# A three-round token-mixing kernel: crossbar transposes issued from ScalarE, rows of x added at an earlier visit, later chunks convolved one step sooner

## The chip, the cores and the metric

The kernel runs on one core of one Trainium2 chip. The metric is device time in microseconds, from the first to the last work of one execution. Timed runs give a median; a profiled execution gives the trace that is read below. Engines are named as the profile names them: PE (TensorE), DVE (VectorE), ACT (ScalarE), POOL (GpSimd), SP (SyncE, which here only issues DMAs).

## The reference

A causal convolution with softmax weights along the sequence is followed by a mixing block. B is 8, S is 4224, D is 192, there are 8 heads of 24 channels and 7 taps.

```python
w = softmax(weight, axis=-1)                      # 8 heads x 7 taps
x = einsum('hk,bskhg->bshg', w, windows_of(x))    # causal window of 7 tokens
theta = x @ w_theta
zr, zi = x * cos(theta), x * sin(theta)
y = einsum('ts,bsd->btd', w_tok_r, zr) + einsum('ts,bsd->btd', w_tok_i, zi)
u = x + y
out = u + maximum(u @ w_ch, 0)
```

Almost all of the arithmetic is in the two 4224 x 4224 token matrices, each multiplied with a 4224 x 1536 operand (8 batches of 192 channels).

## The kernel before, in words

**Tiles.** The sequence is cut into 33 chunks of 128 source tokens (index k) and 33 blocks of 128 target tokens (tb). Batch and channel together are one row of N = 1536 values. A chunk's operand z has seven pieces of 768 columns, since the two token products of a pair of target blocks are computed with seven products in place of eight (a Strassen-like scheme; T1, T2, T3 and T4 are differences of the cosine and sine products).

**Rounds and steps.** 11 chunks (NW) are resident at a time. There are 58 steps. A step works on one pair of target blocks (every seventeenth step on a single one) with all resident chunks. Seventeen steps (NU) visit all target blocks once and the steps go round them a little over three times, so each target block is visited three or four times; between visits its partial sum `pv` is stored in HBM (`part`) and loaded again (`load_rows`, L346). The last visit of a block is its final one. Chunks of the next round replace those of the last one gradually: chunks 11 to 21 enter at steps 18 to 23, chunks 22 to 32 at steps 36 to 41.

**A step.** `mix` (L404) runs seven products ("runs") one after another; each run is 2 matmuls of 384 columns for each resident chunk (L417). With 9 chunks a run has 18 matmuls, with 11 it has 22. After each run `give` (L374) adds the PSUM result to `pv` on DVE (L382); in the first round part of it is copied by ACT (L380). The PSUM results live in tiles `y`, of which there are two buffers.

**The hand-written order.** All other work is a list of events with positions from 0 to 7 within the step, where the integer part is the run. `mix` emits an event when the matmul at that position comes. Each engine executes its instructions in the emitted order (`pe`, `dve`, `act`, `pool` tie each to the one before). DMAs that SP issues, and those of `load_chunk`, are ordered by the tile framework. Events that matter here:
- `w_tasks` (L335): for the following step, four 32x32 block transposes of weight tiles (`turn`, L317) and four sums of them (`wsum`, L329) on DVE, into `wt` tiles with 10 buffers.
- `load_w` (L297): POOL loads the weights of the step after next, with a cast to fp16.
- `load_chunk` (L272): x of a chunk into `xw`, from POOL, and a halo of earlier tokens from SP (L183). `xw` and `pv` share six buffers (tag `big`).
- `conv` (L197): the convolution by PE (L205) in two halves, each evacuated by ACT; x then lies in pieces T2 and T4 of the chunk's z tile and is also stored in HBM as `xs` (L222).
- `transpose` (L226): for each half, six PE transposes (L162) and an evacuation by ACT (L148).
- `theta` (L231): the channel mix by PE (L138), then cosine and sine by ACT (L242). `product` (L247) and `sums` (L253) on DVE finish z.
- `add_x` (L358): before a final visit, the row of x is added to `pv`. Usually SP loads the row into `xr` (L363) and POOL adds it (L364). For some steps (`ahead`) POOL instead issues accumulating DMAs from `xs` to `part` some steps before (L369).
- `outputs` (L456): after a final visit each block is cast to fp16 in two halves (`cast`, L436, ACT), transposed (`turn_u`, L440), mixed with w_ch by PE (L138), joined by DVE (L446) and stored (L451). In steps 41 to 52 the transpose is a crossbar DMA that SP issues (L156); in the last five steps (`late`) PE does it. Times in `outputs` are microseconds relative to the step's end, by the planner's own reckoning of a step.

For a chunk of a later round all ten of its tasks (two convolutions, two transposes, two thetas, two products, two sums) stand in the one step before it enters, at positions 0.1 to 3.7 for the first chunk of a pair and 2.3 later for the second.

Of the kernel before, what the change touches and what calls it, by code (L numbers as in the profile page):

```python
# [16 lines left out]
def kernel(  # L17
# [23 lines left out]
    nc = tc.nc  # L41
# [108 lines left out]
    def turned():  # L150
        return wk.tile([P, 6, P], F16, name="uT", tag="uT", bufs=4)

    def crossed(u):

        uT = turned()
        nc.sync.dma_start(out=uT, in_=u, transpose=True)  # L156
        return uT

    def transposed(u, by_dve=False):
        tp = banks("tp", F16)  # L160
        for k in range(6):
            pe(nc.tensor.transpose(  # L162
                tp[:, 0, k * P : (k + 1) * P], u[:, k * P : (k + 1) * P], ident
            ))
        uT = turned()
        evacuate(uT[:, :, :].rearrange("p k s -> p (k s)"), tp[:, 0, 0 : 6 * P], by_dve)
        return uT
# [3 lines left out]
    class Chunk:  # L171


        def __init__(self, k, before=None):
            self.k = k
            self.xT = {}
            self.xw = wk.tile([2 * WR, 2, B, D], F16, name="xw", tag="big", bufs=6)
            for a in range(NQ):
                h, lo = a // 2, (a % 2) * WR
                t0 = token(k, a)  # L180
                hist = self.xw[lo : lo + HALO, h, :, :]
                if before is not None:
                    nc.sync.dma_start(  # L183
                        out=hist, in_=before.xw[lo + Q : lo + Q + HALO, h, :, :]
                    )
                elif t0 == 0:
                    nc.vector.memset(hist, 0.0)
                else:
                    lo, t0 = lo - HALO, t0 - HALO
                lo += HALO  # L190
                n = (a % 2 + 1) * WR - lo
                nc.gpsimd.dma_start(  # L192
                    out=self.xw[lo : lo + n, h, :, :],
                    in_=x[:, t0 : t0 + n, :].rearrange("b s d -> s b d"),
                )

        def conv(self, j):  # L197

            if j == 0:
                self.z = zpool.tile([P, 7, HN], F16, name="z", tag="z")  # L200
                self.x = self.z[:, T2 : T2 + 2, :].rearrange("p t n -> p (t n)")
            pc = banks("pc")
# [23 lines left out]
        def transpose(self, g):  # L226
            self.xT[g] = transposed(
                self.x[:, g * GC : (g + 1) * GC], 0 < self.k < 3 or (self.k, g) == (0, 1)
            )

        def theta(self, g):  # L231
            v = channel_mix(self.xT[g], wth).rearrange(
# [24 lines left out]
        def tasks(self):  # L257
# [3 lines left out]
            for g in range(NG):  # L261
                yield lambda g=g: self.transpose(g)
# [19 lines left out]
    class Step:  # L282


        def __init__(self, t):
# [7 lines left out]
            self.ahead = self.late or 0 <= t + NU - NSTEP < 2  # L293
            self.time = 0.324 * self.n * (7 if self.pair else 4)
            self.st, self.w, self.ub, self.uT, self.pv = {}, {}, {}, {}, []

# [15 lines left out]
        def wtile(self):  # L312
            return wpool.tile([P, NW, NQ, Q], F16, name="wt", tag="wt", bufs=10)
# [120 lines left out]
        def cast(self, i, g):  # L434
            self.ub[i, g] = wk.tile([P, GC], F16, name="ub", tag="ub", bufs=2)
            act(nc.scalar.activation(  # L436
                out=self.ub[i, g], in_=self.pv[i][:, g * GC : (g + 1) * GC], func=AT.Copy
            ))

        def turn_u(self, i, g):  # L440
            self.uT[i, g] = (transposed if self.late else crossed)(self.ub[i, g])

        def output(self, i, g):
# [3 lines left out]
                out=ub, in0=channel_mix(self.uT[i, g], wch), scalar=0.0, in1=ub,  # L447
# [8 lines left out]
        def outputs(self):  # L456

            found = []
            for i in range(len(self.tbs)):
                if self.late:  # L460
                    at = 1.2 if i or not self.pair else 0.6 - self.time / 7
                    every, turn, mix = 2.0, 1.2, 3.6
                else:
                    at = (8.5 if i else 0.9 - self.time / 7) if self.pair else 0.7
                    every, turn, mix = 3.6, 1.7, 9.0
# [13 lines left out]
    def step_events(t):  # L479
        found = []  # L480
        s = steps[t]
        if t + 1 < NSTEP:
            found += steps[t + 1].w_tasks()
            found.append((1.6, steps[t + 1].load_rows))
            if steps[t + 1].final and not steps[t + 1].ahead:
                for i in range(len(steps[t + 1].tbs)):
                    found.append((3.3 + 1.7 * i, lambda i=i: steps[t + 1].add_x(i)))
        for s in steps[t:]:
            if s.ahead and t == s.t - (4 if s.late else 10):
                for i in range(len(s.tbs)):  # L490
# [9 lines left out]
        if t >= NU - 2:  # L500
            new = [k for k in range(NK) if start[k] == t + 2 and k >= NW]
            for k in new:
                found.append((4.5, lambda k=k: load_chunk(k)))
            at = 0.1
            for k in (k for k in range(NK) if start[k] == t + 1 and k >= NW):
                pos = [0, .5, 1.3, 1.6, 2.1, 2.5, 3.1, 3.15, 3.4, 3.6]

                def add(at, j, k):
                    def go():
                        if j == 0:  # L510
                            chunks[k].todo = chunks[k].tasks()
                        next(chunks[k].todo)()
                    found.append((at, go))
                for j, p in enumerate(pos):
                    add(at + p, j, k)
                at += 2.3
# [188 lines left out]
```

## Time and profile before

| what | value |
|---|---|
| median of 8 runs | 1466.77 us (1462.76 to 1470.15) |
| the profiled execution | 1464.96 us, of which the span from first to last instruction is 1463.2 us |
| step with 11 chunks and no other PE work (rounds one and two) | 25.0 us |
| step in which two chunks enter | 26.7 us |
| step with outputs | 28.2 us |
| crossbar transposes (L156, SP) | 48 of 128 x 768, median 5.5 us from issue to landing |
| POOL adds of x (L364) | 20, 3140 ns each |
| accumulating DMAs for x (L369) | 26 |

The profile's page lists busy time by engine, then groups of instructions, each with its number, its busy time, the mean time of one and the idle time of the engine just before it, with what ended that idle time. The answers on waits give an engine, the line that waited and what released it, then the total in microseconds, the number of waits and the longest. The answers on windows give the busy time of each engine in a stretch.

The steps' times come from the starts of the L417 matmuls, counted off by the number that each step has. From step 4 to step 16, and from 23 to 34, PE does nothing but these matmuls, at 162 ns from start to start.

### The profile page before, as it was taken

How to read it: one execution, taken by the hardware profiler on the slowest of the kernel's cores; microseconds unless marked ns; L12 is line 12 of the kernel's file. 1: busy time of each engine (PE TensorE's matmuls, PEld its weight loads, DVE VectorE, ACT ScalarE, POOL GpSimd, SP SyncE). 2: the span in 40 equal slices, each digit the busy share in tenths (PEclk: the TensorE clock that was granted, in tenths of full speed). 3: DMA queues.
4: the chain of work that ended last, by engine and by line, in shares of the span. 5: the costliest groups of instructions: out<-in, count | busy, mean ns of one | idle time of the engine just before them, and what ended most of it. 6: DMA issues, size and time to landing. Idle time of an engine off the chain costs nothing.

```text
span 1463.2 us, 23889 instructions
## 1 busy us (share of the span) xinstructions
PE 1420.8 (97%) x9807; PEld 888.1 (61%) x9807; DVE 996.6 (68%) x1050; ACT 324.2 (22%) x413; POOL 429.0 (29%) x659
## 2 busy tenths in 40 slices
PE   7889999999999999999999999999999999998997
PEld 4556666666666666666666656666566666665665
DVE  6884645454548687766666657868787788776676
ACT  6861111111124254000000005346001100110134
POOL 7422211111223332211112223332234343454210
PEclk9999999999999999999999999999999999999999
DMA  9976757474699999887779989999899999999983
GB/s 171 222 163 147 143 97 153 88 151 93 136 237 218 219 238 251 201 210 153 216 153 229 223 178 235 193 221 254 178 205 217 228 221 214 221 256 240 239 218 124
DMA packets 273374, 283.57 MB, mean 194 GB/s; under 512 B 107504, under 2 KB 241008, under 8 KB 273264
## 3 DMA queue, kind: packets, MB, share of 16 engines
q0 software_dynamic: 163616, 95.30, 49.0%
q1 hardware_dynamic: 109648, 186.75, 39.4%
q8 instruction: 77, 1.26, 0.3%
q14 instruction: 33, 0.27, 0.1%
HBM read 245.49 MB, written 111.28 MB: 244 GB/s over the span
## 4 chain that ended last, share of the span: by engine, by line
PE 80%; DVE 8%; DMA 7%; ACT 2%; issue 2%; POOL 0%; SPq 0%; DVEq 0%; ACTq 0%
PE y L417 72%; PE v L138 4%; DVE pv L382 2%; DMA xw<-in_x_dram 2%; DVE wt L329 2%; DMA out_dram<-pv 2%; DVE wt L317 2%; PE pc L205 1%; ACT z L242 1%; PE tp L162 1%; DVE pv L446 1%; DMA uT<-ub 1%; DMA xw<-xw 1%; DVE z L253 1%; DVE z L247 1%
## 5 line engine op out<-in xcount | busy, mean ns | idle before, releaser
L417 PE MATMUL y<-z,wt 128*128 128x384 f16 x7656 | 1291.1, 326 | 11.5 <-DVE pv L382 10.5
L417 PEld LDWEIGHTS <-wt 128*128 128x128 f16 x7656 | 740.2, 98 | 487.2 <-issue 17.4
L382 DVE TENSOR_TENSOR pv<-y,pv 128x768 f32<-128x768 f32 x324 | 308.5, 953 | 361.1 <-PE y L417 335.3
L317 DVE STREAM_TRANSPOSE wt<-st 128x1408 f16<-128x1408 f16 (+7 forms) x224 | 326.6, 1464 | 24.9 <-PE y L417 19.7
L304 POOL DMA_DIRECT2D st<-in_moe_w_tok_i_dram x232 | 132.5, 579 | 494.2 <-DVE wt L317 470.3
L304 POOL DMA_DIRECT2D st<-in_moe_w_tok_r_dram x232 | 133.6, 598 | 433.6 <-DVE wt L317 418.3
L329 DVE TENSOR_TENSOR wt<-wt 128x1408 f16<-128x1408 f16 (+7 forms) x216 | 200.2, 927 | 21.8 <-PE y L417 18.2
L148 ACT ACTIVATE z<-pc 128x768 f16<-128x768 f32 x65 | 52.9, 813 | 386.5 <-PE pc L205 386.5
L436 ACT ACTIVATE ub<-pv 128x768 f16<-128x768 f32 x66 | 53.7, 838 | 351.1 <-DVE pv L382 274.4
L380 ACT ACTIVATE pv<-y 128x768 f32<-128x768 f32 x66 | 53.6, 813 | 281.6 <-PE y L417 281.6
L138 PEld LDWEIGHTS <-uT 128*128 128x128 f16 x1056 | 91.1, 98 | 30.6 <-issue 8.8
L192 POOL DMA_DIRECT2D xw<-in_x_dram x132 | 76.1, 584 | 37.0 <-DMA st<-in_moe_w_tok_r_dram 8.8
L446 DVE SCALAR_TENSOR_TENSOR pv<-v,pv 128x768 f32<-128x768 f32 x66 | 62.4, 947 | 27.2 <-PE v L138 21.4
L148 ACT ACTIVATE uT<-tp 128x768 f16<-128x768 f16 x79 | 63.3, 813 | 65.3 <-PE tp L162 65.3
L253 DVE TENSOR_TENSOR z<-z 128x768 f16<-128x768 f16 x132 | 73.4, 556 | 3.8
L364 POOL TENSOR_TENSOR pv<-pv,xr 128x1536 f32<-128x1536 f32 x20 | 62.8, 3140 | 34.2 <-DMA xr<-xs 25.2
L242 ACT ACTIVATE z<-v,half_pi 128x768 f16<-128x768 f32 x66 | 59.5, 902 | 41.5 <-PE v L138 41.4
L247 DVE TENSOR_TENSOR z<-z 128x1536 f16<-128x1536 f16 x66 | 60.4, 951 | 11.6 <-ACT z L242 11.6
L138 PE MATMUL v<-wch,uT 128*128 128x192 f16 x528 | 54.2, 246 | 7.4 <-DMA uT<-ub 5.0
L138 PE MATMUL v<-wth,uT 128*128 128x192 f16 x528 | 55.0, 248 | 3.1 <-ACT z L242 3.0
L242 ACT ACTIVATE z<-v 128x768 f16<-128x768 f32 x66 | 53.1, 805 | 0.0
L162 PE MATMUL tp<-ident,z 128*128 128x128 f16 x396 | 33.7, 223 | 8.1 <-ACT z L242 7.6
(43 smaller groups left out, 158.2 us busy)
## 6 DMA issues: line engine op xcount, KB each, us to landing
part<-pv SPq DMA_DIRECT2D x79, 768.0 KB, 4.1
pv<-part SPq DMA_DIRECT2D x79, 768.0 KB, 5.5
out_dram<-pv SPq DMA_DIRECT2D x66, 384.0 KB, 5.4
st<-in_moe_w_tok_r_dram POOLq DMA_DIRECT2D x136, 176.0 KB, 6.1
st<-in_moe_w_tok_i_dram POOLq DMA_DIRECT2D x136, 176.0 KB, 4.9
xs<-z SPq DMA_DIRECT2D x132, 96.0 KB, 4.6
xw<-in_x_dram POOLq DMA_DIRECT2D x121, 96.0 KB, 6.0
part<-xs POOLq DMA_DIRECT2D x26, 384.0 KB, 8.6
```

What stands on the lines that cost most here:

```text
L138: pe(nc.tensor.matmul(v[:, k, b * D : (b + 1) * D], lhsT=tT[:, 3 * k + b + i, :], rhs=w[:, 2 * b + i, :], start=(i == 0), stop=(i == 1),))
L148: act(nc.scalar.activation(out=out, in_=in_, func=AT.Copy))
L192: nc.gpsimd.dma_start(out=self.xw[lo : lo + n, h, :, :], in_=x[:, t0 : t0 + n, :].rearrange("b s d -> s b d"),)
L242: act(nc.scalar.activation(**args))
L247: dve(nc.vector.tensor_tensor(out=o, in0=xv, in1=o, op=ALU.mult))
L253: dve(nc.vector.tensor_tensor(out=z[:, o, :], in0=z[:, a, :], in1=z[:, b, :], op=ALU.subtract))
L304: pool(nc.gpsimd.dma_start(out=st[a * Q : (a + 1) * Q, 0:nb, :, 0:n] .rearrange("i r bt s -> i (r bt) s"), in_=w[self.tbs[0] * P : (self.t ...
L317: dve(nc.vector.transpose(self.w[name][:, 0 : self.n, :, :], self.st[int(name[1])][:, int(name[0]) - 1, :, 0 : self.n * Q] .rearrange("p b ...
L329: dve(nc.vector.tensor_tensor(out=self.w[name][:, 0 : self.n, :, :], in0=self.w[a][:, 0 : self.n, :, :], in1=self.w[b][:, 0 : self.n, :, : ...
L382: dve(nc.vector.tensor_tensor(out=o, in0=yv, in1=o, op=ALU.add))
L417: pe(nc.tensor.matmul(y[cn][:, q, 0:BH], lhsT=self.w[wn][:, c, :, :].rearrange("p bt i -> p (bt i)"), rhs=chunks[k].z[:, zn, q * BH : (q + ...
L446: dve(nc.vector.scalar_tensor_tensor(out=ub, in0=channel_mix(self.uT[i, g], wch), scalar=0.0, in1=ub, op0=ALU.max, op1=ALU.add,))
```

## The change

1. `crossed` takes a whole block or chunk of 128 x 1536 in one crossbar DMA, and ACT issues it (`nc.scalar.dma_start`), in ACT's order. It is used for u of the non-late final steps (`cross_u`, behind the two casts) and, newly, for the chunks of later rounds (`cross`, in place of two times six PE transposes with their evacuations). The tiles `uT` and `ub` hold a whole row of 1536; `uT` has two buffers instead of four halves. `wt` has nine buffers instead of ten.
2. x of a later chunk is put in an `ub` tile, and its z tile is allocated at `theta`.
3. `add_x` of a block is done in the first visit from step 24 to 34 whose step comes after all tokens of the block have been convolved; only where there is none is it done in the last visit. By the code that is 14 rows in steps 24 to 34, 10 in steps 43 to 52 (all by POOL), and 9 in the late steps by accumulating DMAs as before.
4. Chunks are loaded at position 0.1 (not 4.5), and convolved and crossed from position 4.2 on in that same step, one step sooner than before; theta, products and sums stay in the step before the chunk enters, at positions 1.5 to 3 for the first and 1.7 later for the second.
5. In the final steps the casts come at 1 us intervals, the crossing 2 us after the first cast, the two outputs at 10.5 and 13.3 us after it; block 1 begins 4 us after the step's end instead of 8.5.

```diff
+        return wk.tile([P, 12, P], F16, name="uT", tag="uT")
+    def crossed(uT, u):
+        act(nc.scalar.dma_start(out=uT, in_=u, transpose=True))
...
-            if j == 0:
+            if j == 0 and self.k < NW:
                 self.z = zpool.tile([P, 7, HN], F16, name="z", tag="z")
                 self.x = self.z[:, T2 : T2 + 2, :].rearrange("p t n -> p (t n)")
+            elif j == 0:
+                self.x = wk.tile([P, N], F16, name="ub", tag="ub", bufs=2)[:, :]
...
+        def cross(self):
+            self.xT = turned()
+            crossed(self.xT, self.x)
...
-            for g in range(NG):
-                yield lambda g=g: self.transpose(g)
+            yield self.cross
...
+            visits = [v for v in range(NU, NSTEP) if v % NU == t % NU]
+            self.adds = []
+            for i, tb in enumerate(self.tbs):
+                at = [v for v in visits if self.known(tb) < v - 1 and v + NU < NSTEP
+                      and NU + 1 + base[-1] < v <= 2 * NU]
+                at = at[0] if at else visits[-1]
+                if t == at:
+                    self.adds.append(i)
...
-            return wpool.tile([P, NW, NQ, Q], F16, name="wt", tag="wt", bufs=10)
+            return wpool.tile([P, NW, NQ, Q], F16, name="wt", tag="wt", bufs=9)
...
+                if not self.late:
+                    at = (4 if i else 0.9 - self.time / 7) if self.pair else 0.7
+                    for g in range(NG):
+                        found.append((at + g, lambda i=i, g=g: self.cast(i, g)))
+                        found.append((at + 10.5 + 2.8 * g,
+                                      lambda i=i, g=g: self.output(i, g)))
+                    found.append((at + 2, lambda i=i: self.cross_u(i)))
+                    continue
...
-            if steps[t + 1].final and not steps[t + 1].ahead:
-                for i in range(len(steps[t + 1].tbs)):
+            if not steps[t + 1].ahead:
+                for i in steps[t + 1].adds:
                     found.append((3.3 + 1.7 * i, lambda i=i: steps[t + 1].add_x(i)))
...
+        for i, k in enumerate(entering(2)):
+            found.append((0.1 + 0.5 * i, lambda k=k: load_chunk(k)))
+            for at in (4.2, 4.6, 5.1):
+                add(k, at + i)
+        for i, k in enumerate(entering(1)):
+            for at in (1.5, 1.9, 2.5, 2.55, 2.8, 3):
+                add(k, at + 1.7 * i)
```

## The prediction

> **What bounds the kernel now.** I read the page first, then TensorE's waits, the groups of instructions, and tables of busy time by stage.
>
> ```profile
> span 1463.2 us, 23889 instructions
> ...
> PE 1420.8 (97%) x9807; PEld 888.1 (61%) x9807; DVE 996.6 (68%) x1050; ACT 324.2 (22%) x413; POOL 429.0 (29%) x659
> ...
> PE y L417 <- DVE pv L382: 10.5, 16, 1.8
> ...
> PE v L138 <- DMA uT<-ub: 5.0, 4, 2.8
> ...
> L162 PE MATMUL tp<-ident,z 128*128 128x128 f16 x396 | 33.7, 223 | 8.1 <-ACT z L242 7.6
> ```
>
> TensorE (PE) is busy 97% of the span and hardly waits. The next lines are a middle step of rounds two and three with two entering chunks (529.7 to 556.4 us), the half step with the last two chunks (1006.7), and a plain step (647.4); columns: length, then busy us of PE, PEld, DVE, ACT, POOL, clock, DMA share.
>
> ```profile
> 529.70:556.40 26.70, 26.70 (x216) 17.20 (x214) 21.90 (x28) 12.66 (x16) 8.37 (x16) 1.00 0.98 236
> 1006.70:1025.30 18.60, 18.12 (x162) 11.83 (x160) 16.88 (x19) 12.34 (x16) 3.91 (x7) 1.00 1.01 310
> ...
> 647.40:672.50 25.10, 25.10 (x157) 15.11 (x155) 16.20 (x15) 0.00 (x0) 4.55 (x8) 1.00 0.77 183
> ```
>
> Where chunks enter, PE never pauses, but VectorE (DVE) is at 82 to 91% and the DMA engines at 98 to 101%: two followers close behind. Half-step 1006.7 and its successor are the place where DVE was already late (0.8 us of the wait above). In the output steps (1051 to 1368 us) PE waits 5.0 us for crossed u and 4.1 us for DVE.
>
> **What the skill says.** "DMA: Bandwidth & Descriptors", section "Issuing engines are not separate DMA queues": DMAs of all issuing engines run on the same 16 engines; another issuer saves only sequencer time. So moving the crossbar transposes to ScalarE (ACT) creates no bandwidth. Its "Queues, rings and completion order" says that each engine takes turns between the queue rows packet by packet: ACT's own row no longer stands behind SP's stores, but shares turns with the POOL queue. In the trace, SP's landings range from 2.5 to 15.5 us, which fits a row that queues. "SBUF — State Buffer", "Who interferes with whom": a VectorE instruction with two SBUF inputs contends with a GpSimd instruction that reads SBUF. The trace agrees: wt sums at L329 of 0.87 us take 3.65 us beside the 3.1 us POOL add.
>
> **Part 1: chunks (steps 16 to 22 and 34 to 40).** 22 later chunks lose two groups of six PE transposes. From the start of such a group to the next group's start is 0.335 us, so PE sheds 44 x 0.335 = 14.7 us. ACT loses 44 evacuations of 0.81 us, DVE nothing. The convolutions (2 x 0.45 us) are moved to the preceding step; their number is the same.
>
> DVE's work, however, does not shrink, and it is now bunched: products and sums of chunk one at positions 2.5 to 3 of 7, of chunk two at 4.2 to 4.7. DVE is in order, and behind the bunch stands the evacuation L382 that the PE run after next needs (y has two buffers). I follow its lateness, with durations from the DVE timeline of 529.7: evacuation 0.88 pitch, turn 1.3, weight sum 0.65, product 0.87, sum of z 0.55 each. A PE run is 18 x 0.1625 = 2.93 us, plus 0.66 for each channel mix and 0.45 for each convolution inside it.
> - Run 2: DVE has 0.88+0.65+1.3+1.74+1.1 = 5.67 against 3.59: 2.1 late.
> - Run 3: 0.88+1.1+1.3 = 3.28 against 4.25: 1.1 late.
> - Run 4: 0.88+1.3+1.74+2.2 = 6.1 against 3.83: 3.4 late.
> - Run 6 wants that evacuation, finished 3.4+1.1 us after run 4; run 5 covers 3.83: PE waits 0.65 us.
>
> Steps 17, 20, 21, 35, 38 each wait so; 18 and 36 take in one chunk, so run 5 lacks 0.9 us of convolution and one of run 4's cover stays: 2.0 each; 22 takes in none: 1.6; 19 and 37: 0.25. Step 40 is worst. DVE has 8 weight jobs for step 41 (10.0 us), three evacuations (2.7) and two chunks (7.9), 20.6 us; PE had 18.6 us and now has 11.7 + 2.6 = 14.3. Its third run's evacuation is 6.8 late, run 3 covers 2.9, and step 41 begins with a wait of about 4.95. Sum: 5 x 0.65 + 4.0 + 1.6 + 0.5 + 4.95 = 14.3. The same reckoning for the code of before gives 0.7, 0.7, 0.7 and 0.8 in steps 19, 37, 40, 41, and the trace has 0.73, 0.73, 0.48, 0.80; so I trust it. Minus these 2.9, DVE takes back about 11.2 of 14.7 us. Net -3.5.
>
> The crossed chunk: ACT issues one transpose of 128x1536 after its second evacuation, and the next chunk's evacuations and Sin stand behind it. From that issue to theta, PE has 11.2 us for chunk one (0.98 of run 4, runs 5, 6, 0, part of 1, the two convolutions, less 1.0 for the evacuation), 13.6 us for chunk two. Nearest row: two 768-column halves on SP, issue 1.22 us each; first issue to second landing about 6.3 us (1133.74 issue; second at 1135.69 with landing 4.2 to 4.9). Bounds 4.5 and 14 us, as the entering chunks' x and the weights fill the POOL row, and some halves needed over 13 us there (below). I take 9 us, a cost of +1.5 us in all, mostly step 40, where the budget is about 9 us. Cover gone: every microsecond over budget costs 1 us a chunk.
>
> **Part 2: output steps 41 to 53.** 48 transposes on SP become 24 double ones on ACT, behind casts that ACT has idle time for (it is busy 3.3 us of 28). SP loses 48 issues and its waits for casts (64 us), so loads of pv and rows xr are no longer stuck behind them. Block 0: casts follow the run-5 evacuation, the transpose is issued about 0.8 us before the step's end, the first output channel mix stands 7.84 us after it: budget 8.65 us. Block 1: over 12 us.
>
> ```profile
> L156 SPq DMA_TRANSPOSE uT<-ub x2: 1217/1284/1351, 1133.7 to 1135.7; - x2
> ...
> DMA to landing us min/median/max: 4.2/4.5/4.9
> ...
> L156 SPq DMA_TRANSPOSE uT<-ub x2: 1326/2868/4411, 1314.2 to 1315.6; - x2
> ...
> DMA to landing us min/median/max: 11.8/13.6/15.5
> ```
>
> The first pair is block 0 of an ordinary step, the second block 1 of step 51, crowded by SP's stores and POOL's accumulating DMAs. I take 6.5 us for block 0: no wait as a rule. Today PE loses 9.0 us in steps 42 to 52: 0.35 a step where the POOL add blocks a weight sum, 5.0 for uT in 51 and 52. Half of the adds leave these steps, and the last output moves from 21.1 to 17.3 us, out of the crowded end: I leave 5 x 0.35 + 1.3 = 3 us. Gain 6.0; bounds 0 and 8.
>
> **Part 3: adding x.** 14 rows go to steps 24 to 34, 10 stay, and the four of steps 41 and 42 become POOL adds of 3.14 us instead of accumulating DMAs. The receiving steps have DVE at 16.2 of 25.1 us; a blocked sum of 2.8 us fits. POOL's weight loads stand behind the add for up to 8 us, with over 15 us in hand. 0 to 3 us; I take +0.5 (a slip of DVE near step 23, where 12.9 us of its work already fill 14.3).
>
> **Edits at nothing.** Ten wt buffers to nine: counting tiles, at most nine live (at positions 2.2 and 3.05), each freed by a run whose evacuation DVE has already waited for. Whole ub and uT tiles hold the same halves; x of a later chunk in ub is released by the products, before the next pair's convolution. Chunk loads at 0.1 instead of 4.5 get 12 us instead of 7.5 before their convolution. If nine buffers were short, each short step would cost a turn, 1.6 us; taken 0.
>
> **Sum.** -14.7 + 11.2 + 1.5 - 6.0 + 0.5 = -7.5 us. Own time of the profiled execution 1464.96 (span 1463.2 and 1.8 around it), so 1457.5; the median of eight, 1466.77, lies 1.8 higher, so I forecast 1459.3.
>
> **Rivals.**
> - DVE absorbs the bunch (say, because PE's runs are longer than their floor): -14.7 + 2.9 + 1.5 - 6 = about -17: 1450; with no landing waits, 1446. For it: DVE's total, 21.9 us, is under the new 25.4 us step. Against: the order is fixed, and the reckoning hits the four old waits. 17%.
> - The landing eats the rest: a chunk lands at 11 to 12 us (+6) and the output steps gain nothing: about 1466, no change. For it: the DMA share of 0.98 to which 2 x 2 us of packets a step are added. 13%.
> - Slower: the double transpose for block 0 lands later than its 8.65 us. Place: first output mix of 12 steps, PE in order, so all later matmuls slip. Price: 12 x (landing - 8.65). The other terms give -9, so it decides from a landing of 9.4 us on; at 10.7 us, with the chunks' waits of +5, the time is 1487, at 10 us about 1476. For it: 13.6 us landings above, and the double size. Against: those stood in SP's row, and around the step's start at 1135.8 POOL issues no load between 1130.4 and 1142.4. 25%.
>
> **Chances.** Forecast 45%, its own range 1453 to 1463. About 0.2% (2.9 us) is what can be told apart. Faster: 43 of the forecast's 45, 17 of the first rival, 2 of the second: 0.62. Same: the other 2 and 11: 0.13. Slower: 0.25. Range 1446 to 1478: it leaves out the far ends of the first and last case.
>
> **What would show it.** L162 falls from 504 to 240 matmuls. In steps 17 to 22 PE's gaps come before run 6, released by DVE pv, 0.6 to 2 us; a gap near 5 us opens at the start of step 41 after a step 40 of some 14.3 us. uT waits in output steps near 0; L329 with 3 us durations now also in steps 23 to 33. I am wrong if steps with chunks last 25.3 us without DVE waits, if PE's longest waiter is uT, or if ACT's Sin comes late behind its own issues.

## The result, and the profile after

The changed kernel takes 1519.03 us (median of 11 runs, 1508.40 to 1537.64) against 1466.58 us for the kernel before beside it: ratio 1.0343, interval 1.0322 to 1.0364. It is 52 us slower, where I forecast a gain of 7.5. Ratios, here and below, leave out executions more than 1.5% above the fastest of their kernel; medians have them all. The profiled executions, 1516.88 and 1464.96 us, are 51.9 us apart. Lines of the page of the changed kernel:

```profile
span 1515.1 us, 23255 instructions
...
PE 1421.9 (94%) x9543; PEld 878.9 (58%) x9543; DVE 1014.9 (67%) x1050; ACT 289.0 (19%) x369; POOL 434.8 (29%) x655
...
q10 hardware_dynamic: 72128, 18.09, 10.0%
```

PE lost 264 matmuls, the 44 groups of six transposes, as it should. It is busy for as long as before (1420.8) in a span 52 us longer. q10 is new: ScalarE's own queue of crossings. In the answer on PE's waits (engine, line and what it reads; the releaser; total us, number, longest) the order has turned:

```profile
PE v L138 <- DMA uT<-ub: 30.6, 11, 9.8
PE y L434 <- DVE pv L399: 18.1, 17, 5.3
PE pc L202 <- DMA xw<-in_x_dram: 14.7, 6, 7.3
...
PE pc L202 <- DMA xw<-xw: 3.6, 4, 1.5
```

Waits for crossed u or x have grown from 5.0 to 30.6 us. Waits for xw, the convolution's input, hardly existed (0.3 us); they are 18.3 now. The one line on xw in the answer for the kernel before, 400 to 1060 us:

```profile
PE pc L205 <- DMA xw<-in_x_dram: 0.3, 1, 0.3
```

The prediction had named "PE's longest waiter is uT" as a sign of being wrong. This is the time by steps, counted off by the L434 matmuls (L417 before), in us of the profiled executions:

| steps | before | after | |
|---|---|---|---|
| 0 to 15 | 374.2 | 376.3 | |
| 16 to 23 (chunks enter) | 199.6 | 213.2 | +13.6 |
| 24 to 33 | 250.2 | 254.0 | +3.8 |
| 34 to 40 (chunks enter) | 177.7 | 201.4 | +23.7 |
| 41 to 52 (outputs) | 343.1 | 351.2 | +8.1 |
| 53 to 57 | 89.4 | 90.1 | |

The loss is where the crossings are, above all where they are new. The chunks' crossings of steps 34 to 40, from the answer on line L155 (duration of the issue, then DMA from issue to landing):

```profile
L155 ACTq DMA_TRANSPOSE uT<-ub x11: 1676/3482/5697, 885.7 to 1045.8; - x11
...
DMA to landing us min/median/max: 4.7/13.7/16.9
```

The median landing is 13.7 us (11.1 in steps 16 to 23), where I took 9 against budgets of 11.2 and 13.6. What stands behind it can be seen on SP, whose waits in 880 to 1060 us are:

```profile
SPq L219 <- ACT ub L148: 26.1, 10, 8.6
SPq L219 <- DMA uT<-ub: 25.1, 5, 7.7
SPq L178 <- DMA uT<-ub: 18.7, 3, 9.8
```

SP's stores of x (L219) and copies of halos (L178) do not read uT, and yet wait 43.8 us for its landing; in the same steps of before no SP wait names uT. The trace shows why. SP and ScalarE signal the completion of their DMAs by the same eight semaphores (POOL has eight of its own), and in none of 1153 cases in this trace was a semaphore given to the next DMA before the last one on it had landed. Step 39, the worst (+13.1 us), shows the chain in the timelines of SP and POOL (start, duration, engine, line; in brackets the idle time before it):

```profile
1001.94 14.56 SPq L219 DMA_DIRECT2D xs<-ub  x8
1016.59 0.93 SPq L447 DMA_DIRECT2D part<-pv  x2
1017.69 11.48 SPq L178 DMA_DIRECT2D xw<-xw  x8
...
1027.26 2.28 POOL L187 DMA_DIRECT2D xw<-in_x_dram  x4 [13.87 <-DMA part<-pv]
```

Eight stores, normally issued as fast as x is ready, take SP 14.6 us: the seventh has the semaphore of a chunk's crossing, which lands at 1015.71 us, 13.8 us after its issue, and is itself issued at 1015.73. The store of pv comes only then and lands after 10.1 us. POOL's load of the next chunk needs that pv's buffer and starts after 13.9 us of waiting; its last piece lands after 12.0 us, and the convolution has then waited 7.3 us.

Each long wait costs more than itself. Busy time by stretch in that step, for the pause and the work behind it (length; busy PE, PEld, DVE, ACT, POOL with instructions; granted clock; DMA share, GB/s):

```profile
1033.65:1040.97 7.32, 0.00 (x1) 0.00 (x2) 0.97 (x2) 0.00 (x0) 0.00 (x0) 0.76 1.14 251
1040.97:1044.20 3.23, 3.23 (x15) 1.53 (x15) 0.00 (x0) 0.81 (x1) 0.00 (x0) 0.50 1.34 173
1044.20:1047.50 3.30, 3.30 (x26) 1.96 (x26) 0.96 (x1) 0.81 (x1) 0.00 (x0) 0.99 1.00 168
```

During the pause PE's clock is halved; in the 3.23 us behind it PE gets 15 matmuls done, then 26 in about as long (7 and 8 of them small ones of the convolution). By the records of the clock PE worked 34.4 us at half clock in the changed kernel and 6.8 before, which costs (34.4 - 6.8) / 2 = 13.8 us. PE is idle for 1515.1 - 1421.9 = 93.2 us of the span, against 42.4 before. The prediction's 14.7 us of shed work would give 50.8 + 13.8 - 14.7 = 49.9 of the 51.9 us. The rest is that less was shed: with half the time at half clock taken off, PE was busy for 1420.8 - 3.4 = 1417.4 us before and 1421.9 - 17.2 = 1404.7 after, 12.7 less.

### The profile page after: what moved, and what is told of

Its sections match the earlier page's. It is cut to its first block, busy times and chain, and to the rows that moved or that the text cites. A ratio compares the mean times of both kernels' runs of the same rounds, so it can differ in the third digit from the quotient of the medians.

```text
span 1515.1 us, 23255 instructions
## 1 busy us (share of the span) xinstructions
PE 1421.9 (94%) x9543; PEld 878.9 (58%) x9543; DVE 1014.9 (67%) x1050; ACT 289.0 (19%) x369; POOL 434.8 (29%) x655
## 4 chain that ended last, share of the span: by engine, by line
PE 70%; DMA 17%; DVE 7%; ACT 3%; issue 2%; POOL 0%; SPq 0%; DVEq 0%; POOLq 0%; ACTq 0%
PE y L434 63%; DMA uT<-ub 11%; PE v L138 4%; DMA xw<-in_x_dram 2%; DVE wt L346 2%; DMA part<-pv 2%; DVE pv L399 2%; DVE wt L334 1%; ACT z L248 1%; PE pc L202 1%; DMA xw<-xw 1%; DVE z L253 1%; DVE z L259 1%; DVE pv L471 1%; ACT uT L148 1%
## 5 line engine op out<-in xcount | busy, mean ns | idle before, releaser
L434 PE MATMUL y<-z,wt 128*128 128x384 f16 x7656 | 1293.6, 328 | 19.0 <-DVE pv L399 18.1
L434 PEld LDWEIGHTS <-wt 128*128 128x128 f16 x7656 | 745.3, 98 | 506.2 <-issue 30.4
L346 DVE TENSOR_TENSOR wt<-wt 128x1408 f16<-128x1408 f16 (+7 forms) x216 | 215.4, 997 | 46.2 <-PE y L434 43.4
L148 ACT ACTIVATE ub<-pc 128x768 f16<-128x768 f32 x44 | 35.1, 810 | 382.9 <-PE pc L202 350.9
L381 POOL TENSOR_TENSOR pv<-pv,xr 128x1536 f32<-128x1536 f32 x24 | 74.8, 3117 | 12.0 <-DMA xr<-xs 9.6
L138 PE MATMUL v<-wth,uT 128*128 128x192 f16 x528 | 57.3, 254 | 17.2 <-DMA uT<-ub 14.7
L138 PE MATMUL v<-wch,uT 128*128 128x192 f16 x528 | 55.6, 250 | 17.7 <-DMA uT<-ub 15.9
L202 PE MATMUL pc<-xw,bands 96*64 96x192 f16 x528 | 37.8, 259 | 20.2 <-DMA xw<-in_x_dram 14.7
L202 PEld LDWEIGHTS <-bands 96*64 96x64 f16 x528 | 22.3, 112 | 41.9 <-issue 23.4
L253 DVE TENSOR_TENSOR z<-ub,z 128x1536 f16<-128x1536 f16 x44 | 39.4, 935 | 1.9 <-ACT z L248 1.9
```

The costliest lines, as they stand in the source:

```text
L138: pe(nc.tensor.matmul(v[:, k, b * D : (b + 1) * D], lhsT=tT[:, 3 * k + b + i, :], rhs=w[:, 2 * b + i, :], start=(i == 0), stop=(i == 1),))
L202: pe(nc.tensor.matmul(pc[half * 2 * Q : (half + 1) * 2 * Q, h // 2, h % 2 * B * G : (h % 2 + 1) * B * G], lhsT=bands[:, 4 * j + h, :, :].r ...
L346: dve(nc.vector.tensor_tensor(out=self.w[name][:, 0 : self.n, :, :], in0=self.w[a][:, 0 : self.n, :, :], in1=self.w[b][:, 0 : self.n, :, : ...
L381: pool(nc.gpsimd.tensor_tensor(out=self.pv[i], in0=self.pv[i], in1=xr, op=ALU.add))
L434: pe(nc.tensor.matmul(y[cn][:, q, 0:BH], lhsT=self.w[wn][:, c, :, :].rearrange("p bt i -> p (bt i)"), rhs=chunks[k].z[:, zn, q * BH : (q + ...
```

## The experiments

The stage times below are always those of the profiled execution, for steps 16 to 23 / 34 to 40 / 41 to 52; before has 199.6 / 177.7 / 343.1, the changed kernel 213.2 / 201.4 / 351.2.

**One part at a time.** Three runs: chunks a step sooner but turned by PE; the outputs part on the kernel before; the adds part on the kernel before.

```diff
# on the changed kernel
-            yield self.cross
+            for g in range(NG):
+                yield lambda g=g: self.transpose(g)
...
-            for at in (4.2, 4.6, 5.1):
+            for at in (4.2, 4.6, 5.1, 5.4):
```

> The changed kernel with one thing undone: the later chunks are turned by PE again (twelve transposes at positions 5.1 and 5.4, evacuated by ACT), still convolved a step sooner. Theory L (late landing of the chunks' crossbar transposes, which PE waits for in order, with the half clock that follows): the chunk steps 16 to 23 and 34 to 40, now 37 us above before, fall to about before plus 4, so the total is about 1519 - 33 = 1486 us. Theory B (the earlier loads: xw waits for a buffer that the store of pv frees, and the convolution waits for xw, crossing or not): PE's waits for xw stay at about 18 us, and the total stays above 1505 us. Theory V (DVE's bunching, which the prediction put at 11 us): DVE waits of 5 us in step 41 stay, the rest of the excess too.

Measured: 1492.15 us, ratio 1.0149 (1.0090 to 1.0208); 202.5 / 183.0 / 355.9. Between 400 and 1060 us PE waits for one thing only:

```profile
PE y L435 <- DVE pv L400: 13.5, 10, 5.3
```

No wait for uT or xw is left, though the loads and convolutions are as early as in the changed kernel. So the waits for xw are a consequence of the crossing. It costs 10.7 + 18.4 = 29.1 us over turning by PE, and PE's relief of 12.7 to 14.7 is in that: 42 to 44 us for 22 chunks. Of DVE's 13.5 us, 3.1 stand in steps 25 to 32, which receive adds; the other 10.4 stand where the chunks' work was moved, although PE sheds none here, so they come from the new positions and not from the crossing.

```diff
# on the kernel before: the outputs part alone
+                    at = (4 if i else 0.9 - self.time / 7) if self.pair else 0.7
...
+                        found.append((at + g, lambda i=i, g=g: self.cast(i, g)))
+                        found.append((at + 10.5 + 2.8 * g,
+                                      lambda i=i, g=g: self.output(i, g)))
+                    found.append((at + 2, lambda i=i: self.cross_u(i)))
...
-            return wpool.tile([P, NW, NQ, Q], F16, name="wt", tag="wt", bufs=10)
+            return wpool.tile([P, NW, NQ, Q], F16, name="wt", tag="wt", bufs=9)
```

> Part 2 alone on the kernel before: whole-row crossbar transposes of u from ACT, the new times in outputs, nine wt buffers; chunks and adds as before. As predicted (a gain of 6 us in the output steps): about 1461 us. If the loss of 8 us that the changed kernel shows in steps 41 to 52 belongs to this part: about 1475 us, with waits for uT of 10 us or more in steps 48 to 53.

Measured: 1490.38 us, ratio 1.0162 (1.0096 to 1.0228); 199.5 / 177.2 / 363.7. Steps 24 to 33 take 250.2 us, so nine wt buffers cost nothing. The loss of 20.6 us, and 5.6 more in 53 to 57, stands in few steps: 51 (+14.6), 53 (+6.8), 52 (+3.8). The others are between -0.5 and +1.2.

```diff
# on the kernel before: the adds part alone
-            if steps[t + 1].final and not steps[t + 1].ahead:
-                for i in range(len(steps[t + 1].tbs)):
+            if not steps[t + 1].ahead:
+                for i in steps[t + 1].adds:
```

> Part 3 alone on the kernel before: fourteen rows of x added in steps 24 to 34. If the waits of 0.9 us in steps 28, 29, 32 and 33 come from it alone: +3.8 us there, and in the output steps 1 to 2 us less for the adds that left: about 1469 us. If those waits need the nine wt buffers: no such waits, about 1465 us.

Measured: 1460.16 us (9 runs), ratio 0.9936 (0.9919 to 0.9954): faster than both kernels, than the one before by 0.6%. 199.5 / 177.2 / 336.6; steps 24 to 33 give up 2.9 us, the output steps win 6.5.

**What in the chunk's crossing costs.** The next kernels add to the one turned by PE a crossing into a tile that nobody reads, issued by ScalarE or by SyncE. Then SyncE issues the crossings that are used, of chunks alone or all, and at last ScalarE issues the chunks' in halves.

```diff
# on the run of chunks turned by PE; in the second run nc.sync.dma_start
+        def cargo(self):
+            spare_uT = wk.tile([P, 12, P], F16, name="xr", tag="xr", bufs=1)
+            crossed(spare_uT, self.x)
```

> As e1_chunks_by_pe, but ACT issues each chunk's crossbar transpose as well, at the same place, into a tile that nobody reads: its traffic and its issue stay, its wait is gone. Theory L: within 4 us of e1_chunks_by_pe. Theory C (the traffic itself delays the loads of x and of the weights, the DMA engines being full): 15 us or more above e1_chunks_by_pe, with PE waits for xw and st.

> As e6_cargo, with the unread transposes issued by SP: traffic alone, with neither a wait for the data nor ACT standing in the issue. Theory C (traffic): within 10 us of e6_cargo, that is above 1520 us. If ACT's standing was e6_cargo's 43 us: within 8 us of e1_chunks_by_pe, about 1495 us.

Measured: from ScalarE 1535.20 us, ratio 1.0419 (1.0354 to 1.0484), 229.9 / 205.2 / 355.1. PE waits 16.5 us for ScalarE's evacuations, which stand behind the issue. From SyncE 1499.61 us, 1.0197 (1.0127 to 1.0266), 211.2 / 187.3 / 336.9: the chunk steps are 13.0 us above those turned by PE, with waits for xw of 11.6 us. Neither run prices the traffic alone. There is one spare tile, so the second crossing of a pair is issued only when the first has landed (in the run from SyncE nine times, 0.02 to 0.07 us after the landing), and its engine stands until then. SyncE's line on it, 400 to 1060 us:

```profile
SPq L233 <- DMA xr<-ub: 39.4, 9, 6.2
```

So the 13.0 us are the traffic and this wait together.

```diff
# on the changed kernel; in the second run in `crossed`, so for outputs too
-            crossed(self.xT, self.x)
+            nc.sync.dma_start(out=self.xT, in_=self.x, transpose=True)
```

> The changed kernel, but the chunks' transposes are issued by SP (those of u stay with ACT). If ACT standing in its own issue (up to 5.7 us, with the next chunk's evacuations behind it) costs the 29 us that the chunk steps lose against e1_chunks_by_pe: steps 16 to 23 and 34 to 40 fall by 15 us or more, total near 1500 us. Theory L (late landing, from whatever queue): as the changed kernel or worse, about 1520 us, with uT waits in steps 17 to 21 and 35 to 40, since SP's row now has the stores of xs ahead.

> The changed kernel with every crossing, of chunks and of outputs, issued by SyncE. Theory 'a second queue for the crossings and ScalarE's order are the price': the two savings measured apart add up, 29 us in the chunk steps and some 17 us in the output steps, so about 1473 to 1478 us; no uT wait over 5 us in steps 51 to 53. Theory 'the volume of crossed data at the end is the price': the chunk steps gain as before, the output steps stay at some 351 to 355 us, and the time is about 1490 us.

Measured: chunks by SyncE 1490.44 us, 1.0170 (1.0127 to 1.0213), 205.9 / 184.9 / 355.0; all by SyncE 1492.55 us, 1.0181 (1.0149 to 1.0214), 202.0 / 183.7 / 356.5. In the chunk steps ScalarE as issuer costs 23.8 us by the first, 28.9 by the second. The second's landings in 410 to 1060 us are near my 9, and SP's waits for uT are 0.4 us in all:

```profile
L155 SPq DMA_TRANSPOSE uT<-ub x22: 1509/3253/6352, 419.9 to 1018.0; - x22
...
DMA to landing us min/median/max: 4.6/9.3/13.1
```

Its chunk steps take 385.7 us, as long as with PE's transposes (385.5): crossing from SyncE uses up PE's relief, and the 29 us come with ScalarE as issuer. The output steps of these two runs take as long from either issuer. With the landings mostly out of the way the second run shows DVE's share bare; three answers on waits, for 508.8 to 587 us (steps 20 to 22), 882 to 936 (35, 36) and 1038.6 to 1066 (41):

```profile
PE y L434 <- DVE pv L399: 2.6, 3, 1.7
...
PE y L434 <- DVE pv L399: 2.6, 2, 2.1
...
PE y L434 <- DVE pv L399: 5.0, 1, 5.0
```

The prediction had 2 x 0.65 + 1.6, 0.65 + 2.0 and 4.95.

```diff
-            crossed(self.xT, self.x)
+            for g in range(NG):
+                crossed(self.xT[:, 6 * g : 6 * g + 6, :], self.x[:, g * GC : (g + 1) * GC])
```

> The changed kernel, each chunk's crossing issued by ScalarE as two halves of 768 columns, both behind the second convolution. Theory 'the size of one transpose is what makes it land late': the waits for uT and xw in steps 16 to 40 fall by half or more, and the time by 15 us or more, to 1500 or less. Theory 'the second queue, and what waits for its landings, is what costs': chunk steps stay within 8 us of the 414.6 of the changed kernel (213.2 + 201.4), SyncE still waits for uT, and the time is 1510 to 1530.

Measured: 1505.87 us, 1.0270 (1.0240 to 1.0299); 216.3 / 193.4 / 344.8. The time lies between the two theories. The chunk steps are at 409.7 against 414.6: within the 8 us of the second, and SP still waits 48.4 us for uT in steps 34 to 40. The size of one transpose explains little of it. What is different with ScalarE as issuer is three things, and no run separates them: the waits on shared semaphores; a third queue beside the others (in the chunk steps POOL's loads of w_tok_i land after a median of 9.3 us, against 6.4 with all crossings by SyncE); and ScalarE's evacuations behind its own issues (SP's stores wait 26.1 us for them in 880 to 1060 us, against 17.8 in 870 to 1040).

**The output steps.** Whole rows by SyncE; halves by ScalarE, each 0.5 us behind its cast; block 1 later; then the accumulating DMAs moved.

```diff
# on the outputs part alone: first run
-        act(nc.scalar.dma_start(out=uT, in_=u, transpose=True))
+        nc.sync.dma_start(out=uT, in_=u, transpose=True)
# second run
-                    found.append((at + 2, lambda i=i: self.cross_u(i)))
+                        found.append((at + g + 0.5, lambda i=i, g=g: self.cross_u(i, g)))
# third run
-                    at = (4 if i else 0.9 - self.time / 7) if self.pair else 0.7
+                    at = (8.5 if i else 0.9 - self.time / 7) if self.pair else 0.7
```

> As e2_outputs_only, but SP issues the whole-row transposes. Theory G (whole rows are the cause: a block's first mix waits for 1536 columns where it waited for 768, and the late one finds the queues full): steps 51 to 53 stay about 20 us above before, total about 1485 to 1490 us. Theory Q (ACT's own queue row is the cause: in the crowded steps its small packets take turns with POOL's for 10 to 20 us): 1465 to 1470 us.

> As e2_outputs_only, but ACT issues two half transposes a block, each half a microsecond behind its cast. Theory G: the first mix needs 768 columns only, steps 51 to 53 come near before, total about 1468 us. Theory Q: no better than e2_outputs_only, about 1488 us.

> The outputs part alone, whole rows issued by ScalarE, with block 1 begun 8.5 us after the step's end, as in the kernel before, instead of 4. Theory 'both blocks' crossings bunched into 6 us beside the loads of pv are what makes them land late': steps 51 to 53 lose their waits of 14.5, 6.5 and 3.2 us, the output steps take 345 us or less, and the time is 1472 or less. Theory 'a whole row behind its two casts on ScalarE's queue lands late beside the accumulating DMAs, whenever block 1 starts': waits for uT over 5 us stay in steps 50 to 53 and the time is 1480 to 1492.

Measured, ratio and steps 41 to 52: by SyncE 1.0059 (1.0040 to 1.0079), 346.7; halves 1.0038 (1.0019 to 1.0058), 353.7; block 1 late 1.0237 (1.0184 to 1.0290), 379.9. Whole rows from ScalarE cost 1.6%, so another issuer or half the size takes away most of the loss but not all, and the times, 1473.37 and 1473.67 us, are those of neither theory; the third run is slower than either of its theories had it. Most of the loss stands in steps 50 to 52 each time, with waits for uT of 4 to 17.6 us (the third run also has some 3 us in 45 and 47). The third run did not do what I meant: ScalarE issues as soon as its casts are done, so the crossings still came 3 to 5 us apart and only the outputs moved. It says nothing about bunching; it shows how widely the same crossings scatter. So do the profiled executions of the changed kernel, of the chunks turned by PE, of the two runs with a spare tile and of chunks by SyncE, which all have the same output code: their steps 41 to 52 take 336.9 to 355.9 us. What runs beside them in the bad steps is in the answer on DMA for step 52 of the changed kernel, 1384 to 1400 us (queue: packets, MB, share; then issues with their median us to landing):

```profile
q10 hardware_dynamic: 1683, 0.42, 57.8%
q0 software_dynamic: 998, 1.09, 52.1%
q1 hardware_dynamic: 144, 0.79, 18.7%
...
part<-xs POOLq DMA_DIRECT2D x2, 384.0 KB, 22.0
st<-in_moe_w_tok_r_dram POOLq DMA_DIRECT2D x4, 112.0 KB, 20.2
uT<-ub ACTq DMA_TRANSPOSE x1, 25.4
```

All three queues are busy, they move 145 GB/s against 192 over the whole span, and all that is issued there lands after 20 us or more. `part<-xs` are the accumulating DMAs of the last five steps' rows of x, issued in steps 49 to 53 before and after alike. Two runs move them.

```diff
# on the outputs part alone; 10 in one run, 2 in the other
-            if s.ahead and t == s.t - (4 if s.late else 10):
+            if s.ahead and t == s.t - (2 if s.late else 10):
```

> The outputs part alone (whole rows from ScalarE, which took 363.7 us in steps 41 to 52 and 1490 in all), with the accumulating DMAs of the last five steps' rows issued ten steps ahead instead of four, so in steps 43 to 47 and not 49 to 53. Theory 'a whole row lands late where the accumulating DMAs run beside it': the waits for uT over 4 us leave steps 50 to 53 and stand, shorter or not, in 44 to 48. Theory 'the crossings are late by their own size, wherever these DMAs run': waits over 4 us stay in steps 50 to 53, and the output steps take 355 us or more.

> The outputs part alone (whole rows from ScalarE), with the accumulating DMAs of the last five steps' rows two steps ahead. Theory 'what this part costs is the crossings beside those DMAs': steps 41 to 50 without a uT wait over 2 us, steps 41 to 52 at 336 to 346 us, the time 1461 to 1474. Theory 'a whole row also lands late without them': uT waits over 3 us in several of the steps 43 to 50, steps 41 to 52 at 350 or more, 1478 us or more.

Measured: ten steps ahead, ratio 1.0072 (1.0041 to 1.0103), with executions from 1469.5 to 1507.0 us and a median of 1486.02; the profiled one took 1498.69. The waits have moved with the DMAs: 14.9 us in step 45, 14.4 in 46, 6.3 still in 50, none over 1 in 51 to 53. (A run below that has the same edit beside SyncE's halves has its longest wait for uT in step 45 too, 9.8 us; its profiled execution, 1470.95 us, is close to its median.) Two steps ahead: 1459.37 us, ratio 0.9955 (0.9934 to 0.9976), 199.5 / 179.4 / 334.2. The waits for uT from 1050 to 1420 us in the outputs part alone, then with the DMAs ten and two steps ahead (one line of each):

```profile
PE v L138 <- DMA uT<-ub: 30.3, 7, 14.5
```
```profile
PE v L138 <- DMA uT<-ub: 38.1, 5, 14.9
```
```profile
PE v L138 <- DMA uT<-ub: 2.0, 2, 1.1
```

So a crossing lands late where the accumulating DMAs run beside it, and without them this part costs nothing. The output steps take 8.9 us less than before, but that isn't shown to be a gain of the new crossings: the same move of the DMAs on a kernel with the old crossings (the last two runs below) takes 8.3 us off these steps, 338.6 to 330.3.

**The adds.** What the adds cost in steps 24 to 33 is seen in the run of the adds alone, step 29 (DVE and POOL in the timeline):

```profile
730.14 4.53 DVE L341 TENSOR_TENSOR wt<-wt 128x1408 f16<-128x1408 f16 x1
730.81 3.11 POOL L376 TENSOR_TENSOR pv<-pv,xr 128x1536 f32<-128x1536 f32 x1
```

A weight sum of 0.87 us takes 4.53 beside an add, and PE waits 0.8 us. POOL runs ahead of the planner's positions: the add starts right after the weight load issued ahead of it, just when S3 is due. Four runs move it.

```diff
# on the adds part alone
-                    found.append((3.3 + 1.7 * i, lambda i=i: steps[t + 1].add_x(i)))
+                    found.append((4.35 + 0.02 * i, lambda i=i: steps[t + 1].add_x(i)))
# first run also
-                xr = wk.tile([P, N], F16, name="xr", tag="xr", bufs=1)
+                xr = wk.tile([P, N], F16, name="xr", tag="xr", bufs=2)
# third and fourth run
+                    at = 4.35 + 0.02 * i if s.pair else 3.3 + 1.7 * i
# third run also
-            if s.ahead and t == s.t - (4 if s.late else 10):
+            if s.ahead and t == s.t - 10:
```

To hold the second xr buffer the first run has nine wt buffers.

> The kernel before with the third part alone, nine wt buffers, two xr buffers, and the adds placed behind the second weight load (4.35) instead of in front of it. Theory 'a POOL add blocks the weight sum beside it, and that is all that the adds cost': steps 24 to 33 fall from 253.1 to 250.3 us, the 0.3 us waits of steps 43 to 52 go too, about 1456 us, ratio 0.991. Theory 'nine wt buffers or the later add cost more than the blocking': a new DVE or POOL wait at the start of steps 25 to 34, and 1460 us or more.

> The kernel before with the third part alone, ten wt buffers and one xr buffer as in the run of the adds alone, and the adds placed behind the second weight load (4.35). With one buffer the second row of x loads only after the first add, so the two adds stand some 7.7 us apart and one of them meets S4, none S3. Theory 'only an add that meets S3, or two in a row, delay a PE run': the waits of 0.8 us in steps 28 to 33 go, steps 24 to 33 take 250.3 to 251 us, and the time is 1456 to 1458 us, ratio near 0.991. Theory 'any blocked sum costs, wherever it stands': steps 24 to 33 stay at 253 or more and the time at 1460 or more.

> The kernel before with the third part alone, its adds at 4.35 except behind the half step 23, where they stay at 3.3 and 5.0, and the accumulating DMAs of the last five steps' rows issued ten steps ahead instead of four. Theory 'the waits in steps 28 to 33 come from adds that meet S3, those in 50 to 53 from accumulating DMAs beside the crossings': steps 24 to 33 at 250.3 us, 41 to 52 at 333 to 335, about 1455 us, ratio 0.991. Theory 'these waits only move': 1459 us or more, ratio 0.994 or above.

> The kernel before with the third part alone, adds at 4.35 except behind the half step 23, and the accumulating DMAs where they were (four steps ahead, in 49 to 53). Theory 'a wait for uT follows the accumulating DMAs, a wait for DVE follows an add that meets S3': steps 24 to 33 at 250.2 us as in the run before, the 12 us wait of step 45 gone, steps 41 to 52 at 335 to 340, so 1456 to 1461 us. Theory 'the adds behind the second weight load cost in the output steps': 41 to 52 over 342 and 1462 or more.

Measured: with two xr buffers 1471.16 us, ratio 1.0032 (1.0020 to 1.0044), steps 24 to 33 at 259.9. The timeline of step 28 says why:

```profile
720.95 7.56 DVE L341 TENSOR_TENSOR wt<-wt 128x1408 f16<-128x1408 f16 x1
721.59 6.16 POOL L376 TENSOR_TENSOR pv<-pv,xr 128x1536 f32<-128x1536 f32 x2
```

Both adds now run back to back and hold S4 for 7.6 us. With one buffer: 1461.89 us, 0.9972 (0.9963 to 0.9982); in the profiled execution, at 1471.10 us the longest of 22, steps 25 to 33 are free of waits, but step 24, behind the half step, waits 5.7 us. With that step left as it was, steps 24 to 33 take 250.2 us, exactly those of before. The third run, which also sent the accumulating DMAs ten steps ahead, still took 1470.60 us, 1.0023 (1.0008 to 1.0038): step 45 takes 13.5 us longer than before, 9.8 of them a wait for uT. The fourth left them four ahead: 1456.36 us, 0.9911 (0.9886 to 0.9935).

**The version that beats both kernels.** It is the fourth with those DMAs two steps ahead.

```diff
-            if s.ahead and t == s.t - (4 if s.late else 10):
+            if s.ahead and t == s.t - (2 if s.late else 10):
```

> The same with the accumulating DMAs of the last five steps' rows two steps ahead instead of four, in steps 51 to 55, where only three steps have crossings. Theory 'the waits for uT follow the accumulating DMAs': no uT wait in steps 49 and 50, at most short ones in 51 to 53, steps 41 to 52 at 333 to 336, 1454 to 1457 us, ratio 0.991 or less. Rival: the rows' loads for steps 53 to 57 stand behind the later accumulating DMAs, and steps 53 to 57 take 92 us or more instead of 89.4.

Measured: 1452.76 us, ratio 0.9892 (0.9869 to 0.9916); 199.5 / 177.2 / 330.3, and 90.7 in 53 to 57. Its one wait for uT:

```profile
PE v L138 <- DMA uT<-ub: 1.1, 1, 1.1
```

The rival did not come true. The intervals of this and the fourth run overlap, so the last step is small against the scatter (six executions each, 1451.34 to 1457.31 and 1453.95 to 1459.73 us); against the kernel before the gain of about 1.1% is clear. This version has the kernel before's crossings, by halves from SyncE, and no chunk is crossed.

## Why the prediction was wrong

- **PE sheds 14.7 us**: right in the count, 264 matmuls less, and somewhat high in the price: PE's busy time fell by 12.7 us at equal clock.
- **DVE takes back 11.2 us**: right in mechanism and near in size (the sum itself is off by 0.2: 14.3 - 2.9 is 11.4). Its waits in the run with all crossings by SyncE are 5.0 us in step 41 (forecast 4.95), 1.7 in 22 (1.6), 2.1 in 36 (2.0), 1.5 in 18 (2.0), 0.5 in 20, 21 and 35 (0.65), 0.3 in 19 and 37 (0.25) and none in 17 and 38 (0.65): 12.2 us in all for 14.3. In the changed kernel step 41 waits 5.3 us; in 20, 21 and 35 a wait for uT or xw comes first and hides DVE's. One of the four old waits by which I trusted the reckoning, the 0.48 us in step 40, was not DVE's: the answer for 1006 to 1052 us puts it down to ACT's Sin.
- **The crossed chunk costs 1.5 us**: the step that failed most. It cost 42 to 44 us. I sized the landing (9 us) from halves on SP's queue and compared it with PE's budget alone. The median was 11.1 and 13.7 us, and three things were not in the sum: what else waits for that landing (43.8 us of SP's waits in steps 34 to 40, and through them, as in step 39, PE's waits for xw, 18.3 us in all), that some other transfers land later beside ScalarE's queue (9.3 us against 6.4 for w_tok_i), and the half clock behind long pauses (13.8 us over the whole run). The rival "the landing eats the rest" had the landing, 11 to 12 us, and by the same budget priced it at +6. I had cited from the Trainium skill, "DMA: Bandwidth & Descriptors", section "Issuing engines are not separate DMA queues", that another issuer saves only sequencer time. The runs agree that nothing is gained; here it lost: 24 to 29 us in these steps for the same crossings from ScalarE.
- **Outputs gain 6.0 us (0 to 8)**: wrong in sign, by a term left out. Alone this part lost 20.6 us in the output steps. I named the crowded end and supposed that the last output leaves it; what crowds it, the accumulating DMAs in steps 49 to 53, stays where it is and meets the crossings of block 0. Their budget of 8.65 us was near: it came out as 7.5 us where the crossing was issued only 0.7 to 0.8 us into the next step, and 9.0 elsewhere (changed kernel and outputs part alone). Away from the accumulating DMAs the loss is gone; that the crossings themselves gain is not shown.
- **The slower rival** had the right place, the first output mix waiting for a whole row, and a wrong price. It is not 12 x (landing - 8.65): most landings fit (median 6.5 us in 1050 to 1420), and in the bad executions one to three late ones, landing after 12 to 27 us, cost 3 to 18 us each. And it missed the chunks, where 37.3 of the 51.9 us lie.
- **Adds cost 0.5 us (0 to 3)**: wrong in sign, as I had excluded a gain without a reason. Alone they save 9.4 us (0.0064 x 1466; the two profiled executions are 4.3 apart). I had booked the relief of the output steps to part 2. The cost, 2.9 us, is in the range, but comes from S3 under the add, not from a slip near step 23.
- **Edits at nothing**: nine wt buffers and the sooner loads of chunks cost nothing by themselves. The sooner loads do make POOL dependent on SP's store of pv, which is how the crossing reached xw.
- **Half clock**: the trace of before had one such window behind a wait of 2.84 us. The Trainium skill states it too: "TensorE: Matmul & The Clock Gate", section "What's actually happening", has half the clock after an idle window of about 3.4 us. The trace agrees on the half and the window, but shorter pauses are enough (below). A wait of over 2.5 us, which I priced at its length, as a rule costs 1.3 to 2.9 us more: between start and end of the twenty runs PE worked 2.7 to 5.9 us at half clock in each such stretch.

## What to carry to other kernels

A DMA's landing is not only for its reader: list everything issued after it that can wait for its completion, on every queue, before you compare the landing with a budget. In stages whose DMA share was near 1.0 already, added crossings landed after 9.3 us from one issuer and 11.1 to 13.7 from another, so a landing measured in a quiet stage is no price there. Look first at what runs beside a late landing, since moving one group of DMAs by two steps was worth more here than the choice of issuer or size. And book a gain to the edit that makes it: the adds, run alone, were the one part of the three that gained.

## What the runs showed of the hardware

- Behind the first 45 us, the twenty traces have 52 pauses of PE longer than 2.45 us. All but one (3.39 us) were followed by a stretch at half clock of 3.41 us or a multiple. Of 20 pauses of 1.96 to 2.45 us, 8 were; of shorter ones a single one, of 1.84 us, which came 1.3 us behind another of 1.27. In the first 45 us a pause of 1.8 us was enough in 11 traces of 20.
- Packets of a crossing (256 bytes) took 17.7 ns each on average when one ran alone (1097.8 us). In the window of step 52 above it was 0.578 x 16 x 16 us / 1683 = 88 ns, beside the other two queues. The issue of a whole row took ScalarE 1.3 us at best and 12.7 us in step 52; 21.4 us in one other run.
- Beside one POOL add a DVE sum with two SBUF inputs took 3.6 to 4.5 us in place of 0.87, and beside two adds in a row 7.6 us: the sum did not end between them. The Trainium skill, "SBUF — State Buffer", "Who interferes with whom", has the conflict; that it spans two instructions is what the trace adds.
